# All low parts of the fp32r splits on VectorE instead of GpSimd, in a fused recurrence with two feed-forward networks

## The chip, the cores and the metric

The kernel runs on one core of a Trainium2 chip. The metric is device time of one execution in microseconds, the median of several runs. Engines are called as in the profile: PE is TensorE, DVE VectorE, ACT ScalarE, POOL GpSimd, SP the engine that issues the DMAs.

## The reference

```python
def _attn_ref(q, k, v, a_re, a_im):                # 4 batches, 8 heads, 768 steps, dim 48
    mag = np.sqrt(a_re * a_re + a_im * a_im)
    scale = np.minimum(mag, 0.999) / (mag + 1e-06)
    a_re_n, a_im_n = (a_re * scale, a_im * scale)
    for t in range(S):
        ar, ai = (a_re_n[:, :, t, :, None], a_im_n[:, :, t, :, None])
        new_re = ar * S_re - ai * S_im
        new_im = ar * S_im + ai * S_re
        S_re, S_im = (new_re + kv_t, new_im)       # kv_t: outer product of k and v of step t
        y[:, :, t] = q_t @ S_re

x = y as 3072 tokens x 384
x = (silu(x @ w_gate) * (x @ w_val)) @ w_out       # 384 -> 1536 -> 384
h = x @ w_in                                       # 384 -> 2048
return (h - np.tanh(h)) @ w_out2                   # 2048 -> 384, float32
```

The weights of both networks are drawn as 64-bit floats.

## The kernel before

**Splits.** A number that goes into a matmul of the two networks is held as two fp32r numbers, a high and a low part: ACT casts the value to fp32r (hi), and a subtraction, value minus hi, gives lo. Every product of two such numbers is three matmuls (hi.hi, hi.lo, lo.hi). The program makes a split in three kinds of places:

- `split` (lines 512 to 515) for the middle values: in network 1 after the gate product (L563), once per block of 128 of the 1536 columns and per token tile; in network 2 after `shrink` (lines 566 to 584, h - tanh h by five VectorE instructions L579, L581, L582, L583, L584). The cast is L514, the low part L515 on GpSimd. Only the very last one of the program was on VectorE (L640).
- `decode` (lines 146 to 161) for weights: `words` makes an fp32 out of the two 32-bit words of a double by ACT (L140) and four VectorE instructions in place on one tile (L141 to L144), then ACT casts (L150) and GpSimd subtracts (L152). For the first gate/value blocks TensorE makes the low part by two matmuls instead (L158, L159); that stays.
- The inputs of the networks (L464, L544) had their low part on VectorE already.

**Stages.** (1) Attention in chunks of 128 steps: `group_steps` makes the running products of the complex factors for two units (chunk of one batch) with VectorE products (L266, L268, L269) and a normalisation (squares L229 and the product L250 on GpSimd); `unit_a` and `unit_b` make scores, mask them (for the first eight units by GpSimd, L424), update the state (H products on GpSimd, L413 to L415) and write the unit's output as network 1's input. (2) Network 1 over ten token tiles of 256 (six) and 384 (four) tokens, `moe1_tile`: 12 steps per tile, each with 18 matmuls of the first product and 9 of the second for the step before. The attention of later tiles is put between its steps by `bg`, the decode of w_out in the first tile, and the decode of network 2's weights in the last tile (`dec2`), where raw tiles have three buffers and decoded ones two. (3) Network 2 over eight tiles of 384 tokens, `moe2_tile`: 16 steps per tile, each with 9 matmuls of the first product and 9 of the second, two steps behind. The rest of the decode of its second weights lies beside its first steps.

**The order of the work** is set by a scheduler which simulates the program as it is written and places each instruction in its engine's queue; each queue then runs in order on the chip. So a change of one instruction's engine moves others as well.

Of the kernel before, what the change touches and what calls it, by code (L numbers as in the profile page):

```python
# [8 lines left out]
F32 = mybir.dt.float32  # L9
# [4 lines left out]
ALU = mybir.AluOpType  # L14
# [27 lines left out]
def tile_kernel(ctx: ExitStack, tc: tile.TileContext, q, k, v, a_re, a_im, w_gate, w_val, w_out, w2_in, w2_out, out):  # L42
    nc = tc.nc
    PE, ACT, DVE, POOL, SP = nc.tensor, nc.scalar, nc.vector, nc.gpsimd, nc.sync
    B, H, S, D = q.shape
    NT, DM = out.shape
# [9 lines left out]
    NF2 = FF2 // P  # L56
# [12 lines left out]
    NTOK = 3 * P  # L69
# [58 lines left out]
    def PA(name):  # L128
        pool, tag = banks[0]
        banks.append(banks.pop(0))  # L130
        return pool.tile([P, 512], F32, tag=tag, name=name)
# [5 lines left out]
    def words(raw, t):  # L137

        w, ti = raw.bitcast(I32).rearrange("p (c w) -> p c w", w=2), t.bitcast(I32)
        ACT.activation(out=t, in_=raw.bitcast(F32).rearrange("p (c w) -> p c w", w=2)[:, :, 1], func=AF.Abs)  # L140
        DVE.tensor_scalar(out=t, in0=t, scalar1=W_LO, scalar2=W_HI, op0=ALU.max, op1=ALU.min)  # L141
        DVE.tensor_scalar(out=ti, in0=ti, scalar1=3, scalar2=0x3FFFFFF8, op0=ALU.logical_shift_left, op1=ALU.bitwise_and)  # L142
        DVE.scalar_tensor_tensor(out=ti, in0=w[:, :, 1], scalar=-0x40000000, in1=ti, op0=ALU.bitwise_and, op1=ALU.bitwise_or)  # L143
        DVE.scalar_tensor_tensor(out=ti, in0=w[:, :, 0], scalar=29, in1=ti, op0=ALU.logical_shift_right, op1=ALU.bitwise_or)  # L144

    def decode(raw, hi, lo, t, by_pe=False):

        words(raw, t)
        tv = t.rearrange("p (k c) -> p k c", c=hi.shape[2]) if len(hi.shape) == 3 else t
        ACT.copy(out=hi, in_=tv)  # L150
        if not by_pe:
            POOL.tensor_tensor(out=lo, in0=tv, in1=hi.bitcast(F32), op=ALU.subtract)  # L152
            return

        h2, l2 = (x.rearrange("p k c -> p (k c)") for x in (hi, lo))
        for c in range(0, t.shape[1], DM):
            ps = ps_1.tile([P, 512], F32, tag="l1", name="psL")[:, 0:DM]
            PE.matmul(ps, lhsT=ident, rhs=t[:, c:c + DM], start=True, stop=False)  # L158
            PE.matmul(ps, lhsT=nident, rhs=h2[:, c:c + DM], start=False, stop=True)  # L159
            ACT.copy(out=l2[:, c:c + DM], in_=ps)  # L160
# [346 lines left out]
    def catch_up(lag):  # L507

        while len(pend) > lag:
            pend.popleft()()  # L510

    def split(t, hi, lo, eng=POOL):

        ACT.copy(out=hi, in_=t)  # L514
        eng.tensor_tensor(out=lo, in0=t, in1=hi.bitcast(F32), op=ALU.subtract)  # L515

    def MT(tag, bufs, dt=F32):
        return m1.tile([P, N1], dt, tag=tag, name=tag, bufs=bufs)
# [51 lines left out]
    def shrink(p, t, pool):  # L570


        n = [P, p.shape[1]]
        uu = pool.tile(n, F32, tag="uu", name="uu")
        vv = pool.tile(n, F32, tag="vv", name="vv")
        far = pool.tile(n, I32, tag="far", name="far")
        ACT.activation(out=t, in_=p, func=AF.Tanh)  # L577
        ACT.activation(out=uu, in_=p, func=AF.Square, scale=KSQ)  # L578
        DVE.tensor_tensor(out=p, in0=p, in1=t, op=ALU.subtract)  # L579
        ACT.activation(out=vv, in_=uu, func=AF.Square, scale=1.0 / G_C, bias=gbias)  # L580
        DVE.tensor_scalar(out=far, in0=uu, scalar1=G_C * G_MAX * G_MAX, scalar2=None, op0=ALU.is_gt)  # L581
        DVE.tensor_tensor(out=t, in0=uu, in1=t, op=ALU.mult)  # L582
        DVE.scalar_tensor_tensor(out=t, in0=vv, scalar=G_F, in1=t, op0=ALU.add, op1=ALU.mult)  # L583
        DVE.copy_predicated(out=t, mask=far, data=p)  # L584
# [22 lines left out]
    def moe2_tile(ti, bg):  # L607
        x = ot.pop(ti)
        acc = []

        def l4(f, g):
            if f == 0:
                for n in range(ti * TU2, (ti + 1) * TU2):
                    acc.append((ps_2.tile([P, 512], F32, tag="l2", name="l4") if n % 5 < 3 else PA("l4"))[:, 0:DM])
            for tb in range(TU2):
                for n, (a, b) in enumerate(PASSES):
                    PE.matmul(acc[tb], lhsT=g[a][:, tb * P:(tb + 1) * P], rhs=w2_hl[f][:, b], start=(f == 0 and n == 0), stop=(f == NF2 - 1 and n == 2))  # L617
            if f == NF2 - 1:
                for tb in range(TU2):
                    r = m2.tile([P, DM], F32, tag="res", name="res", bufs=3)  # L620
                    with tc.high_priority():
                        if (ti + 1) * NTOK == NT and tb % 2:
                            DVE.tensor_copy(out=r, in_=acc[tb])
                        else:
                            ACT.copy(out=r, in_=acc[tb])
                    row = ti * NTOK + tb * P
                    SP.dma_start(out=out[row:row + P, :], in_=r)

        for f in range(NF2):
            sl = slice(f * P, (f + 1) * P)  # L630
            pool, tag = (ps_1, "l1") if f % 3 < 2 else (ps_g, "psA")
            p = pool.tile([P, 512], F32, tag=tag, name="l3")[:, 0:NTOK]
            for n in range(3 * NJ):
                kk, (a, b) = n // 3, PASSES[n % 3]
                PE.matmul(p, lhsT=wi_hl[a][:, kk, sl], rhs=x[b][:, kk, :], start=(n == 0), stop=(n == 3 * NJ - 1))  # L635
            catch_up(2)
            t = MT("t", MID)[:, 0:NTOK]
            shrink(p, t, m2)
            g = [MT(tag, MID, F32R)[:, 0:NTOK] if f % (MID + 2) < MID else m2.tile([P, NTOK], F32R, tag=tag, name=tag) for tag in ("hi", "lo")]
            split(t, *g, eng=DVE if (ti + 1) * NTOK == NT and f == NF2 - 1 else POOL)  # L640
            pend.append(lambda f=f, g=g: l4(f, g))
            bg(f)

# [59 lines left out]
    for ti in range(len(TILES)):  # L703
# [11 lines left out]
        def bg(n):  # L715
            if ti == 0:
                dec1(N_PRE + 2 + n)
            if last:
                if n == 2 * N_A:
                    w1a.close()  # L720
                    w2.append(second.enter_context(tc.tile_pool(name="w2a", bufs=1, side="left", reuse_waits="tile")))
                if n < NF2:
                    dec2(n, "i")
                for _ in range(W2STEP):
                    if n >= N0 and len(w2_hl) < N_EARLY + (2 * N_A if n >= 2 * N_A else 0):
                        get_w2()
            prog["credit"] += RATE
            while prog["credit"] >= 1:
                prog["credit"] -= 1
                att_next(goal, SHARE if ti else SHARE1)  # L730
# [170 lines left out]
```

## Time and profile before

| | |
|---|---|
| three runs | 1281.08 us median (1279.9 to 1281.22) |
| the profiled execution | 1280.44 us in all, span 1278.7 us |
| PE busy | 1147.8 us, 90% of the span |
| DVE busy | 1008.1 us, 79%, 1961 instructions |
| ACT busy | 695.3 us, 54% |
| POOL busy | 465.8 us, 36%, 402 instructions |
| DMA | 163.53 MB, 128 GB/s mean |

Busy time is the union of an engine's instructions as the profiler recorded them, from start to end, whatever an instruction did in between. Shares of the whole span are means over stages with different limits, so the rows by stage tell more.

### The profile page before, as it was taken

To read this page: it belongs to the slowest core of one execution; us is meant where nothing else is said; L and a number is where in the kernel's file an instruction comes from. 1 tells how busy PE (TensorE), PEld (TensorE's weight loads), DVE (VectorE), ACT (ScalarE), POOL (GpSimd) and SP (SyncE) were. 2 spreads that over 40 slices of the span, in tenths; PEclk is the share of its full clock that TensorE was granted. 3 is DMA by queue.
4 is the path that set the end of the run, shared out by engine and by line. 5 is a ranking of instruction groups with operands and counts; after the bars stand their busy time and mean duration, and the time that the engine had idled before them with its cause. 6 is when DMAs were issued, how large, how long until landed. Compare 5 with 4: busy or idle time off the path is not lost.

```text
span 1278.7 us, 21147 instructions
## 1 busy us (share of the span) xinstructions
PE 1147.8 (90%) x7512; PEld 1113.6 (87%) x7512; DVE 1008.1 (79%) x1961; ACT 695.3 (54%) x1454; POOL 465.8 (36%) x402
## 2 busy tenths in 40 slices
PE   3346899898999999999999998987999999999997
PEld 2126888898999998999999998877999999999996
DVE  6988988697675849677683328999998899999996
ACT  6454655556545463736534224446666566666664
POOL 0034454333252223233232224544444444444442
PEclk9755979999899999999999999998999999999999
DMA  6586667679676776768565546752101101101000
GB/s 169 141 203 146 145 185 194 158 194 215 158 176 178 183 186 151 184 155 185 160 145 141 147 118 221 235 173 87 57 1 57 38 20 56 38 19 56 1 19 22
DMA packets 282289, 163.53 MB, mean 128 GB/s; under 512 B 155328, under 2 KB 263232, under 8 KB 282176
## 3 DMA queue, kind: packets, MB, share of 16 engines
q1 hardware_dynamic: 282176, 162.10, 48.7%
q8 instruction: 61, 1.00, 0.3%
q14 instruction: 52, 0.43, 0.1%
HBM read 121.26 MB, written 37.86 MB: 124 GB/s over the span
## 4 chain that ended last, share of the span: by engine, by line
PE 53%; DVE 23%; ACT 8%; DMA 8%; issue 4%; POOL 2%; SPq 1%; DVEq 0%; ACTq 0%; POOLq 0%
PE l L617 14%; PE l L635 13%; PE l L554 12%; PE acc L538 5%; PE psS L420 2%; DVE prod L266 2%; DVE t L143 2%; DMA TQ<-qk_d 2%; PE psY L448 2%; DVE PL L268 2%; PE psY L446 2%; DVE t L142 1%; DVE t L583 1%; DVE t L144 1%; DMA raw<-in_moe_w_val_dram 1%
## 5 line engine op out<-in xcount | busy, mean ns | idle before, releaser
L515 POOL TENSOR_TENSOR lo<-t,hi 128x384 fp32r<-128x384 f32 (+1 forms) x247 | 289.4, 1172 | 517.2 <-ACT hi L514 485.7
L554 PE MATMUL l<-x,wgv 128*128 128x256 f32 (+1 forms) x2160 | 366.8, 317 | 21.6 <-DVE t L563 14.6
L554 PEld LDWEIGHTS l<-x,wgv 128*128 128x128 f32 x2160 | 324.4, 197 | 29.4 <-DVE t L563 19.4
L514 ACT CAST hi<-t 128x384 fp32r<-128x384 f32 (+1 forms) x248 | 119.5, 482 | 244.4 <-DVE t L563 141.6
L635 PE MATMUL l<-x,wi 128*128 128x384 f32 x1152 | 223.0, 339 | 8.3 <-DVE t L584 7.2
L635 PEld LDWEIGHTS l<-x,wi 128*128 128x128 f32 x1152 | 202.5, 189 | 9.9 <-DVE t L584 8.3
L617 PE MATMUL l<-w,hi 128*128 128x384 f32 x768 | 188.0, 338 | 0.5 <-ACT hi L514 0.5
L538 PE MATMUL acc<-hi,wo 128*128 128x256 f32 (+1 forms) x720 | 180.0, 312 | 4.0 <-ACT hi L514 2.7
L583 DVE SCALAR_TENSOR_TENSOR t<-vv,t 128x384 f32<-128x384 f32 x128 | 139.8, 1092 | 11.8 <-DVE t L582 0.5
L617 PEld LDWEIGHTS l<-w,hi 128*128 128x128 f32 x768 | 139.5, 189 | 0.8 <-ACT hi L514 0.8
L538 PEld LDWEIGHTS acc<-hi,wo 128*128 128x128 f32 x720 | 127.0, 193 | 5.8 <-ACT hi L514 3.8
L617 PE MATMUL l<-w,lo 128*128 128x384 f32 x384 | 120.2, 337 | 0.0
L563 DVE TENSOR_TENSOR t<-t,l 128x256 f32<-128x256 f32 (+1 forms) x120 | 56.2, 468 | 81.0 <-PE l L554 67.8
L538 PE MATMUL acc<-lo,wo 128*128 128x256 f32 (+1 forms) x360 | 111.3, 315 | 3.8 <-POOL lo L515 3.8
L266 DVE TENSOR_TENSOR prod<-PL 128x384 f32<-128x384 f32 x168 | 111.6, 664 | 3.1
L577 ACT ACTIVATE t<-l 128x384 f32<-128x384 f32 x128 | 62.9, 491 | 50.4 <-PE l L635 48.1
L579 DVE TENSOR_TENSOR l<-l,t 128x384 f32<-128x384 f32 x128 | 72.1, 563 | 13.1 <-ACT uu L578 13.1
L580 ACT ACTIVATE vv<-uu,gbias 128x384 f32<-128x384 f32 x128 | 79.4, 621 | 0.4
L558 ACT ACTIVATE t<-l 128x256 f32<-128x256 f32 (+1 forms) x120 | 51.1, 426 | 51.7 <-PE l L554 50.9
L584 DVE COPY_PREDICATED t<-far,l 128x384 f32<-128x384 int32 x128 | 75.8, 592 | 3.7
L446 PE MATMUL psY<-v,SC 128*128 128x48 f32 x384 | 75.3, 291 | 0.7 <-POOL SC L424 0.6
L538 PEld LDWEIGHTS acc<-lo,wo 128*128 128x128 f32 x360 | 69.2, 192 | 6.0 <-POOL lo L515 5.7
(131 smaller groups left out, 1936.8 us busy)
## 6 DMA issues: line engine op xcount, KB each, us to landing
wo<-wo_d SPq DMA_DIRECT2D x108, 384.0 KB, 3.9
qk_d<-QK SPq DMA_DIRECT2D x24, 768.0 KB, 4.6
raw<-in_moe_w_out_dram SPq DMA_DIRECT2D x28, 384.0 KB, 3.1
TK<-qk_d SPq DMA_DIRECT2D x48, 192.0 KB, 4.2
TQ<-qk_d SPq DMA_DIRECT2D x48, 192.0 KB, 5.1
x<-o_d SPq DMA_DIRECT2D x16, 576.0 KB, 5.2
raw<-in_moe_w_in_dram SPq DMA_DIRECT2D x16, 384.0 KB, 3.8
ar<-in_a_re_dram SPq DMA_DIRECT2D x24, 192.0 KB, 3.8
```

The source lines that it names most:

```text
L266: DVE.tensor_tensor(out=pr, in0=prev.unsqueeze(2).to_broadcast(sh), in1=cur.unsqueeze(1).to_broadcast(sh), op=ALU.mult)
L446: PE.matmul(o, lhsT=SC[h // 4][:, h % 4], rhs=vn[:, D * h:D * (h + 1)], start=True, stop=(c == 0))
L514: ACT.copy(out=hi, in_=t)
L515: eng.tensor_tensor(out=lo, in0=t, in1=hi.bitcast(F32), op=ALU.subtract)
L538: PE.matmul(acc[j], lhsT=w[:, a, j * P:(j + 1) * P], rhs=m[b], start=(f == 0 and i == 0), stop=(f == NF1 - 1 and i == 2))
L554: PE.matmul(p, lhsT=w[a][:, kk], rhs=x[b][:, kk, 0:n_t], start=(n == 0), stop=(n == 3 * NJ - 1))
L579: DVE.tensor_tensor(out=p, in0=p, in1=t, op=ALU.subtract)
L580: ACT.activation(out=vv, in_=uu, func=AF.Square, scale=1.0 / G_C, bias=gbias)
L583: DVE.scalar_tensor_tensor(out=t, in0=vv, scalar=G_F, in1=t, op0=ALU.add, op1=ALU.mult)
L584: DVE.copy_predicated(out=t, mask=far, data=p)
L617: PE.matmul(acc[tb], lhsT=g[a][:, tb * P:(tb + 1) * P], rhs=w2_hl[f][:, b], start=(f == 0 and n == 0), stop=(f == NF2 - 1 and n == 2))
L635: PE.matmul(p, lhsT=wi_hl[a][:, kk, sl], rhs=x[b][:, kk, :], start=(n == 0), stop=(n == 3 * NJ - 1))
```

## The change

`decode` and `split` call VectorE for the subtraction; the argument that chose the engine goes, and with it the exception for the last step. The matmul form of the low part stays, as do the other GpSimd instructions.

```diff
@@ decode
         ACT.copy(out=hi, in_=tv)
         if not by_pe:
-            POOL.tensor_tensor(out=lo, in0=tv, in1=hi.bitcast(F32), op=ALU.subtract)
+            DVE.tensor_tensor(out=lo, in0=tv, in1=hi.bitcast(F32), op=ALU.subtract)
             return
@@ split
-    def split(t, hi, lo, eng=POOL):
+    def split(t, hi, lo):
         ACT.copy(out=hi, in_=t)
-        eng.tensor_tensor(out=lo, in0=t, in1=hi.bitcast(F32), op=ALU.subtract)
+        DVE.tensor_tensor(out=lo, in0=t, in1=hi.bitcast(F32), op=ALU.subtract)
@@ moe2_tile
-            split(t, *g, eng=DVE if (ti + 1) * NTOK == NT and f == NF2 - 1 else POOL)
+            split(t, *g)
```

The scheduler places the moved instructions, and others with them. Three places:

GpSimd's queue at the start, before (wo and wgv are decoded weights of network 1, SC the scores, ar a factor of the recurrence):

```order
L152 TENSOR_TENSOR wo<-dt,wo 128x384
L229 TENSOR_TENSOR s_516<-s_516,s_517 128x768
L152 TENSOR_TENSOR wo<-dt,wo 128x384
L152 TENSOR_TENSOR wgv_143<-dt,wgv_142 128x768
L424 AFFINE_SELECT SC<-SC 128x512
L250 TENSOR_TENSOR ar<-ar,s_516 128x768
L424 AFFINE_SELECT SC<-SC 128x512
L152 TENSOR_TENSOR wo<-dt,wo 128x384
```

and after the change:

```order
L229 TENSOR_TENSOR s_516<-s_516,s_517 128x768
L424 AFFINE_SELECT SC<-SC 128x512 x2
L250 TENSOR_TENSOR ar<-ar,s_516 128x768
L413 TENSOR_TENSOR Hn<-Z,LS 96x384
L414 TENSOR_TENSOR Zs<-Zs,LS 96x384
```

The low parts are gone from it, and both masks of the first unit stand ahead of the normalisation.

VectorE's queue in the last tile of network 1, one step from L563 to L563, before (t_ are tiles under decode, raw_ the raw words):

```order
L563 TENSOR_TENSOR t<-t,l_8964 128x384
L141 TENSOR_SCALAR t_9221<-t_9221 128x384
L142 TENSOR_SCALAR t_9221<-t_9221 128x384
L143 SCALAR_TENSOR_TENSOR t_9221<-raw_9220,t_9221 128x384
L141 TENSOR_SCALAR t_9258<-t_9258 128x384
L144 SCALAR_TENSOR_TENSOR t_9221<-raw_9220,t_9221 128x384
L142 TENSOR_SCALAR t_9258<-t_9258 128x384
L143 SCALAR_TENSOR_TENSOR t_9258<-raw_9257,t_9258 128x384
L563 TENSOR_TENSOR t<-t,l_9026 128x384
```

and after the change, two steps later:

```order
L563 TENSOR_TENSOR t<-t,l_9084 128x384
L144 SCALAR_TENSOR_TENSOR t_9258<-raw_9257,t_9258 128x384
L141 TENSOR_SCALAR t_9269<-t_9269 128x384
L515 TENSOR_TENSOR lo<-t,hi 128x384
L142 TENSOR_SCALAR t_9269<-t_9269 128x384
L152 TENSOR_TENSOR w_9256<-t_9258,w_9256 128x384
L143 SCALAR_TENSOR_TENSOR t_9269<-raw_9268,t_9269 128x384
L144 SCALAR_TENSOR_TENSOR t_9269<-raw_9268,t_9269 128x384
L141 TENSOR_SCALAR t_9292<-t_9292 128x384
L563 TENSOR_TENSOR t<-t,l_9132 128x384
```

Low parts of the middle values and of the weights now stand between the decode's instructions, and a step holds a little less of the decode: when the last L563 is reached, 3 decodes more than before are still to be done, beside the first steps of network 2.

VectorE's queue in the steady loop of network 2, one step, before:

```order
L582 TENSOR_TENSOR t<-uu,t 128x384
L583 SCALAR_TENSOR_TENSOR t<-vv,t 128x384
L584 COPY_PREDICATED t<-far,l_10429 128x384
L579 TENSOR_TENSOR l_10464<-l_10464,t 128x384
L581 TENSOR_SCALAR far<-uu 128x384
```

and after the change:

```order
L582 TENSOR_TENSOR t<-uu,t 128x384
L515 TENSOR_TENSOR lo<-t,hi 128x384
L583 SCALAR_TENSOR_TENSOR t<-vv,t 128x384
L584 COPY_PREDICATED t<-far,l_10429 128x384
L579 TENSOR_TENSOR l_10464<-l_10464,t 128x384
L581 TENSOR_SCALAR far<-uu 128x384
```

The low part of the step before now stands between L582 and L583 of the next one.

## Rows read from the trace of the kernel before

**Rows 1.** Busy time of the engines by stage, us from the span's start
```profile
core 0: us, PE busy (x) PEld busy (x) DVE busy (x) ACT busy (x) POOL busy (x), PEclk, DMA share, GB/s
0.00:135.00 135.00, 63.06 (x246) 46.71 (x246) 106.70 (x222) 72.85 (x139) 32.29 (x30) 0.70 0.65 163
135.00:560.00 425.00, 392.92 (x3159) 385.47 (x3157) 328.76 (x714) 237.80 (x506) 159.73 (x148) 0.95 0.73 179
560.00:764.00 204.00, 203.81 (x1361) 201.75 (x1360) 106.86 (x233) 85.97 (x172) 54.28 (x50) 0.97 0.58 144
764.00:890.00 126.00, 108.40 (x578) 100.71 (x577) 115.23 (x189) 62.78 (x134) 58.30 (x54) 0.97 0.58 188
890.00:1260.00 370.00, 370.00 (x2125) 370.00 (x2125) 342.06 (x593) 230.73 (x495) 158.02 (x119) 1.00 0.09 31
```

**Rows 2.** Groups of GpSimd's instructions by line and shape: busy us, mean ns | idle before
```profile
L515 POOL TENSOR_TENSOR lo<-t,hi 128x384 fp32r<-128x384 f32 x175 | 223.0, 1274 | 359.5 <-ACT hi L514 328.0 <-issue 9.3 <-PE l L635 6.9
L515 POOL TENSOR_TENSOR lo<-t,hi 128x256 fp32r<-128x256 f32 x72 | 66.4, 922 | 157.8 <-ACT hi L514 157.8
```

**Rows 3.** Groups of VectorE's instructions by line, whole span: busy us, mean ns | idle before
```profile
L583 DVE SCALAR_TENSOR_TENSOR t<-vv,t 128x384 f32<-128x384 f32 x128 | 139.8, 1092 | 11.8 <-DVE t L582 0.5
...
L143 DVE SCALAR_TENSOR_TENSOR t<-raw,t 128x384 int32<-128x384 int32 x32 | 29.4, 917 | 1.0
L144 DVE SCALAR_TENSOR_TENSOR t<-raw,t 128x384 int32<-128x384 int32 x32 | 23.6, 738 | 0.7
...
L142 DVE TENSOR_SCALAR t<-t 128x384 int32<-128x384 int32 x32 | 20.8, 651 | 0.7
...
L515 DVE TENSOR_TENSOR lo<-t,hi 128x384 fp32r<-128x384 f32 x1 | 0.6, 559 | 0.6 <-ACT hi L514 0.6
```

**Rows 4.** Timeline of network 2's loop: start us, duration us, engine, line, instruction
```profile
1004.27 0.56 DVE L579 TENSOR_TENSOR l<-l,t 128x384 f32<-128x384 f32 x1
...
1005.01 0.55 DVE L582 TENSOR_TENSOR t<-uu,t 128x384 f32<-128x384 f32 x1
1005.06 1.38 POOL L515 TENSOR_TENSOR lo<-t,hi 128x384 fp32r<-128x384 f32 x1 [1.72 <-ACT hi L514]
...
1005.66 1.19 DVE L583 SCALAR_TENSOR_TENSOR t<-vv,t 128x384 f32<-128x384 f32 x1
...
1007.37 0.56 DVE L579 TENSOR_TENSOR l<-l,t 128x384 f32<-128x384 f32 x1
...
1224.46 0.55 DVE L583 SCALAR_TENSOR_TENSOR t<-vv,t 128x384 f32<-128x384 f32 x1
```

**Rows 5.** Timeline of one step of the decode beside network 1's last tile
```profile
839.55 0.55 DVE L563 TENSOR_TENSOR t<-t,l 128x384 f32<-128x384 f32 x1
840.01 1.21 DVE L142 TENSOR_SCALAR t<-t 128x384 int32<-128x384 int32 x1
...
843.40 0.36 DVE L142 TENSOR_SCALAR t<-t 128x384 int32<-128x384 int32 x1
843.72 1.00 POOL L152 TENSOR_TENSOR w<-t,w 128x384 fp32r<-128x384 f32 x1 [1.64 <-ACT w L150]
843.80 1.34 DVE L143 SCALAR_TENSOR_TENSOR t<-raw,t 128x384 int32<-128x384 int32 x1
...
845.91 0.55 DVE L563 TENSOR_TENSOR t<-t,l 128x384 f32<-128x384 f32 x1
```

**Rows 6.** Timeline of GpSimd at the start
```profile
90.42 6.50 POOL L152 TENSOR_TENSOR wgv<-dt,wgv 128x768 fp32r<-128x768 f32 x1 [4.70 <-ACT wgv L150]
96.86 1.36 POOL L424 TENSOR_SCALAR_AFFINE_SELECT SC<-SC 128x512 f32<-128x512 f32 x1
...
100.26 0.96 POOL L424 TENSOR_SCALAR_AFFINE_SELECT SC<-SC 128x512 f32<-128x512 f32 x1
```

**Rows 7.** Groups of VectorE's instructions by line, 135 to 560 us
```profile
L266 DVE TENSOR_TENSOR prod<-PL 128x384 f32<-128x384 f32 x112 | 76.3, 681 | 2.1
L268 DVE TENSOR_TENSOR PL<-prod 128x96 f32<-128x96 f32 x111 | 44.6, 401 | 1.4
```

**Rows 8.** Instructions of line 268: ns least/median/most, first and last start
```profile
L268 DVE TENSOR_TENSOR PL<-prod x168: 240/256/1896, 31.3 to 666.7; 128x96 f32<-128x96 f32 x168
```

## The prediction

> **What bounds the kernel now.** I read the busy time of each engine by stages first. The reader is to see five stretches with five limits [rows 1]. Up to 135 us TensorE works less than half the time: the first attention units and the first weights are on their way. From 135 to 560 us (the six 256-token tiles) it is busy 392.9 of 425 us, VectorE 328.8. From 560 to 764 it is full (203.8 of 204) and VectorE half idle. From 764 to 890 (the second network's weights are decoded) VectorE is the fullest at 115.2 of 126, and TensorE leaves 17.6 us unused. From 890 on TensorE is busy 370.00 of 370 us with 2125 matmuls, 174 ns each. A step of network 2 has 18 of them, so 3.13 us.
>
> So a change to VectorE and GpSimd can win at most where TensorE is not full: some 72 us in the first stretch, 32 in the second, 17.6 in the fourth, and the end. It can lose anywhere, if VectorE becomes slower than TensorE.
>
> Then I read how long the same VectorE instruction takes at different times. L583 takes 1092 ns on average [rows 3], 1.19 us in the steady loop, but 0.55 us at 1224.46, in a pause of GpSimd's low parts [rows 4]. In the loop it starts at 1005.66 while GpSimd's low part runs from 1005.06 to 1006.44, and it ends at 1006.85, 0.41 us after that part: it stands still behind it. The decode shows the same: L142 takes 0.36 us alone and 1.21 us at 840.01; L143 takes 1.34 us at 843.80, beside a low part that runs to 844.72, and ends 0.42 us after it [rows 5]. The two engines do not work side by side here; an instruction of one waits for one of the other. GpSimd's busy time is thus largely VectorE's too.
>
> **The change part by part.** It removes 294 subtractions from GpSimd (247 of L515 and 47 of L152) and puts them on VectorE. GpSimd needs 1274 ns for the 384-wide and 922 for the 256-wide ones [rows 2]. VectorE has one such instruction in the trace, the last of the program: 559 ns for 384 columns [rows 3]. Independent instructions follow each other faster than they take: L579 at 1004.27 takes 0.56, L582 at 1005.01 takes 0.55, yet L579, L581 and L582 start within 0.74 us [rows 4]. I cost a 384-wide low part at 0.47 us of VectorE's queue, with 0.56 as the upper bound; the 256-wide ones at 0.35, between 256/384 of 0.559 (0.37) less the overlap, and 0.56 above.
>
> *Network 2's loop (890 us to the end).* One VectorE step is L579 to L579, 1004.27 to 1007.37, or 3.10 us [rows 4]: hardly less than TensorE's 3.13. Without GpSimd, L583 falls from 1.19 to 0.55, which returns 0.64; the low part costs 0.47 to 0.56. The step becomes 2.93 to 3.02 us, and the new order puts the low part behind L582, three instructions after the L584 whose result ScalarE casts for it, so that the cast lies beside them. TensorE stays the bound: 0 us for 118 steps. At the very end L583 and L579 of the last step come some 0.5 us sooner: -0.5.
>
> VectorE is busy 342 of 370 us in this stretch [rows 1], so it looks like the engine to take work from. The Trainium skill (Perfetto Trace Analysis, Optimizing Scalar/DVE Operations) says that where VectorE is saturated, moving work to ScalarE or even GpSimd may pay, with the caution that those two share a port. By its first half this change goes the wrong way, and the sum would be that of the second rival below; by the rows of L583 it costs nothing.
>
> *The decode (764 to 890 us).* Here VectorE is the bound, and its own waits behind GpSimd can be counted from the 32 decodes [rows 3]: L142 651 instead of 360 ns (9.3 us), L143 917 instead of 550 (11.7), L144 738 instead of 550 (6.0); the short times are those of L142 at 843.40 and of L583 at 1224.46, which is the same operation on as many columns [rows 4, 5]. Together 27 us come back. Added are the low parts that GpSimd did in this window, 54 instructions [rows 1], at 0.47 us: 25.4 us. The difference is -1.6 us. But the low parts also fill gaps. The decode's four instructions work in place on one tile, so each waits for the one before: L142 at 843.40 takes 0.36 and the next starts 0.40 later, and L143 alone would hold the queue 0.55 to 0.6 us before L144 [rows 5]. The new order puts low parts between them. With some 0.1 us saved at two places of each of 32 decodes, 6.4 us more. I take -7. The bounds: TensorE cannot gain more than the 17.6 us it leaves here, so -17.6; and if the low parts take 0.56 (30.2 us) and a third of them wait 0.5 us for their cast (9 us), +12.
>
> A step of network 1's last tile shows the size: L563 at 839.55 to L563 at 845.91 is 6.36 us [rows 5], against 27 matmuls of 174 ns, 4.70 us, for TensorE. The new order has three decodes fewer before the last L563 than the old one, and so three more beside network 2's first steps; the sum over the whole window holds both.
>
> *The start (0 to 135 us).* GpSimd's low part of a whole gate/value block runs from 90.42 for 6.50 us, and the mask of the first scores (L424) follows it at 96.86, the second at 100.26 behind the normalisation L250 [rows 6]. In the new order the two masks stand first. That can bring the first unit forward by 0 to 6.5 us; six low parts on VectorE (three of them twice as wide) cost 3 x 1.1 + 3 x 0.56 = 5 us at most, beside other work and waits for loads. I take -3, with -6.5 and +5 as bounds.
>
> *The 256-token tiles (135 to 560 us).* Added: 72 low parts of 0.35 and nine of L152 at 0.47, 29 us. Returned: L268 takes 401 ns on average against a median of 256 over the kernel, 111 times, 16.1 us [rows 7, 8]; L266 681 ns against the 559 of the low part that has its size [rows 3, 7], 112 times, 13.7 us. But of GpSimd's 159.7 us here the low parts are 66 to 76 (72 of 922 ns and nine more), under half, and the masks, the H products and the normalisation stay. So some 13 of those 30 us return, and VectorE has some 16 us more to do in a stretch where it idles 96. For it: GpSimd's remaining work no longer queues behind low parts. I take 0, with -10 (a third of TensorE's 32 idle us) and +12.
>
> From 560 to 764 us TensorE is full and VectorE has 97 us to spare for its 20-odd low parts: 0. No DMA is added. GpSimd issues none; SP's stores of the decoded weights wait for VectorE instead.
>
> **The sum**: -0.5 - 7 - 3 + 0 = -10.5 us against the profiled execution (1278.7 us span, 1280.44 in all), 1269.9 us. That execution lies 0.64 under the median of 1281.08, so the same change gives 1270.5 there: I say 1270.
>
> **The rivals.** *One: the gain is only moved.* The decode's raw tiles have three buffers, and a load can start only after the L144 three decodes before. Loads then set the pace, or the three decodes pushed behind the last L563 take back what the earlier steps gained. The decode gives 0, the start 0 to 3: 1277 to 1281. For it: TensorE waits at the border of the two networks for VectorE in any case. Against it: L141 to L144 hardly wait for loads in this trace. Chance 0.13.
>
> *Two: VectorE saturates.* If L583, L142 and L143 are long for a reason of their own, the loop becomes 3.10 + 0.47 = 3.57 us against 3.13, and 118 steps cost 52 us; the decode adds 25: 1357 us. It decides as soon as L583 stays above 1.0 us. The short L583 at 1224.46 speaks against it. The rule on saturated engines would have it so. Chance 0.04.
>
> *Three: VectorE becomes the bound in the 256-token tiles.* Its queue is in order, and a low part waits there for ScalarE's cast, with the attention's products behind it. If the 13 us do not return, since the remaining GpSimd work now hits VectorE instead, 29 us are added, on the path in the share in which VectorE is busy, 329 of 425: +22, less 10.5: 1292 us. It turns to slower when more than 10.5 of the 29 us reach the end. For it: VectorE is on the chain at several places there. Against: 96 us idle. Chance 0.11.
>
> **How the numbers follow.** The forecast has 0.72, of which 0.70 ends faster and 0.02 within 0.2% (2.6 us, about what a measurement of this kernel can tell from no change). Rival one's 1277 to 1281 lies across that line: 0.06 faster, 0.07 same. Rival three: 0.03 same, 0.08 slower; rival two: 0.04 slower. Faster 0.76, same 0.12, slower 0.12. The range: the bounds of decode, start and tiles add to -34 and +29, which won't meet; two of three at the good end give -25 (1255), and toward the other side the range takes in rival one and a little of three, 1284.
>
> **What would show it.** Right: in the steady loop L583 at 0.55 us and the step of TensorE at 3.13; L142 to L144 near 0.36 and 0.55; the stretch from the first decode to the first full step of network 2 shorter by 4 to 12 us; the first masks 2 to 6 us earlier. Wrong: L583 still above 1 us; VectorE at over 95% between 135 and 560 us and TensorE's idle time there above 40 us; or steps of network 2 over 3.2 us.

## The result, and the profile after

The changed kernel takes 1243.89 us (median of 4 runs, 1241.27 to 1248.19), the kernel before beside it 1281.15 us. The ratio is 0.972 with a 95% interval of 0.9689 to 0.9751: 37 us faster. The forecast of 1270 us had the direction right and the size wrong; even its low end, 1255, was too high. The profiled execution took 1244.15 us with a span of 1242.4 us, 36.3 less than before.

The page's first rows, which answer to the table of before:

```profile
PE 1131.6 (91%) x7512; PEld 1100.3 (89%) x7512; DVE 989.9 (80%) x2255; ACT 693.9 (56%) x1454; POOL 124.2 (10%) x108
```

VectorE executes 294 instructions more and is busy 18 us less (989.9 against 1008.1). To see where the 36.3 us lie, both traces have to be cut at the same points of the work, not at the same times. The marks are the starts of VectorE instructions: the first L563 (network 1 begins), the 37th (its fourth tile), the 73rd (its seventh, the first of 384 tokens), the last L464 (the attention's last output), the first L584 (the first finished middle value of network 2) and the last L584. The view of busy time by stretch, of the kernel before, cut there:

```profile
0.00:137.00 137.00, 65.06 (x262) 48.71 (x263) 108.11 (x224) 74.44 (x143) 32.29 (x30) 0.70 0.66 163
137.00:347.70 210.70, 190.46 (x1499) 185.32 (x1499) 170.30 (x367) 124.94 (x263) 86.57 (x80) 0.94 0.72 177
347.70:541.90 194.20, 184.18 (x1532) 182.48 (x1532) 139.19 (x313) 105.03 (x228) 64.13 (x61) 0.97 0.73 180
541.90:764.60 222.70, 220.70 (x1478) 218.03 (x1477) 124.75 (x266) 92.69 (x186) 63.31 (x56) 0.97 0.60 149
764.60:868.40 103.80, 87.66 (x473) 80.59 (x471) 93.99 (x150) 50.85 (x108) 48.95 (x46) 0.99 0.63 205
868.40:1267.00 398.60, 397.15 (x2265) 396.51 (x2266) 370.00 (x642) 245.94 (x527) 170.52 (x129) 0.99 0.11 35
```

And of the changed kernel (columns as in [rows 1]: the stretch, its length, then busy us and instructions of PE, PEld, DVE, ACT and POOL, granted clock, DMA share, GB/s):

```profile
0.00:135.30 135.30, 66.46 (x256) 47.61 (x257) 107.73 (x227) 72.22 (x137) 16.47 (x24) 0.68 0.64 163
135.30:329.30 194.00, 180.68 (x1501) 177.62 (x1501) 165.62 (x400) 118.12 (x253) 46.54 (x36) 0.97 0.76 189
329.30:527.70 198.40, 185.45 (x1544) 181.99 (x1542) 145.91 (x362) 114.71 (x245) 31.68 (x25) 0.98 0.76 182
527.70:747.10 219.40, 217.62 (x1476) 214.64 (x1477) 134.00 (x302) 92.73 (x185) 29.53 (x24) 0.99 0.62 152
747.10:831.60 84.50, 80.67 (x464) 79.75 (x462) 77.35 (x183) 48.56 (x101) 0.00 (x0) 0.99 0.75 238
831.60:1231.80 400.20, 397.68 (x2261) 395.99 (x2262) 357.56 (x786) 246.19 (x533) 0.00 (x0) 0.99 0.11 36
```

The differences are -1.7, -16.7, +4.2, -3.3, -19.3 and +1.6 us, and the work behind the last mark is 1.1 us shorter (11.7 against 10.6): -36.3 together. Two places carry it: the six 256-token tiles of network 1, and the border between the networks, where the weights are decoded. The six tiles are to be read together, -12.5 us, since some of the attention's work has moved across the mark between the third and the fourth: of L347, for example, four instructions stood in the first three tiles, and three do now. At the border TensorE's idle time falls from 16.1 us (103.80 less 87.66) to 3.8, at a granted clock of 0.99 before and after.

The reader is to see VectorE's column. At the border it executes 183 instructions in place of 150 and is busy 17 us *less*. In the six tiles it is 82 instructions more (762 against 680) and only 2.0 us more (311.5 against 309.5). VectorE's groups over the whole span, which answer to [rows 3, 7, 8], show why:

```profile
L266 DVE TENSOR_TENSOR prod<-PL 128x384 f32<-128x384 f32 x168 | 100.1, 596 | 2.9
L515 DVE TENSOR_TENSOR lo<-t,hi 128x384 fp32r<-128x384 f32 x176 | 98.9, 562 | 21.0 <-ACT hi L514 20.9
L583 DVE SCALAR_TENSOR_TENSOR t<-vv,t 128x384 f32<-128x384 f32 x128 | 70.4, 550 | 0.8
...
L515 DVE TENSOR_TENSOR lo<-t,hi 128x256 fp32r<-128x256 f32 x72 | 39.1, 543 | 11.2 <-ACT hi L514 10.9
L143 DVE SCALAR_TENSOR_TENSOR t<-raw,t 128x384 int32<-128x384 int32 x32 | 17.7, 553 | 0.2
L144 DVE SCALAR_TENSOR_TENSOR t<-raw,t 128x384 int32<-128x384 int32 x32 | 17.7, 552 | 0.3
...
L142 DVE TENSOR_SCALAR t<-t 128x384 int32<-128x384 int32 x32 | 11.3, 355 | 0.3
```

L583 is at 550 ns where it was at 1092, L143, L144 and L142 at 553, 552 and 355 where they were at 917, 738 and 651. A low part takes 562 ns here; on GpSimd it took 1274 [rows 2]. In the timeline of VectorE in network 2's loop (which answers to [rows 4]) no instruction is lengthened any more, and a step, from the L579 at 1000.63 to that at 1003.73, has room for 0.41 us of idle time:

```profile
1000.63 0.56 DVE L579 TENSOR_TENSOR l<-l,t 128x384 f32<-128x384 f32 x1
1001.10 0.34 DVE L581 TENSOR_SCALAR far<-uu 128x384 int32<-128x384 f32 x1
...
1002.30 0.54 DVE L515 TENSOR_TENSOR lo<-t,hi 128x384 fp32r<-128x384 f32 x1
1002.77 0.54 DVE L583 SCALAR_TENSOR_TENSOR t<-vv,t 128x384 f32<-128x384 f32 x1
1003.73 0.57 DVE L579 TENSOR_TENSOR l<-l,t 128x384 f32<-128x384 f32 x1 [0.41 <-ACT uu L578]
```

A step of network 1's last tile beside the decode (which answers to [rows 5]; timeline of VectorE, some lines left out) shows every instruction at its short duration, and all but two start before the one ahead has ended. Its length, 4.44 us from L563 to L563, is no measure of the gain against the 6.36 quoted before: the steps of that tile are uneven (0.46 to 6.37 us before, 0.07 to 6.81 after; their means are 3.75 and 4.45 us), and the decode that they hold differs. The border's whole length is the measure.

```profile
799.22 0.55 DVE L563 TENSOR_TENSOR t<-t,l 128x384 f32<-128x384 f32 x1
799.68 0.35 DVE L142 TENSOR_SCALAR t<-t 128x384 int32<-128x384 int32 x1
799.95 0.55 DVE L152 TENSOR_TENSOR w<-t,w 128x384 fp32r<-128x384 f32 x1
800.42 0.55 DVE L143 SCALAR_TENSOR_TENSOR t<-raw,t 128x384 int32<-128x384 int32 x1
800.89 0.55 DVE L515 TENSOR_TENSOR lo<-t,hi 128x384 fp32r<-128x384 f32 x1
...
803.66 0.55 DVE L563 TENSOR_TENSOR t<-t,l 128x384 f32<-128x384 f32 x1
```

### The profile page after: what moved, and what is told of

Same layout as the page of the kernel before. It is cut to its first block, busy times and chain, and to the rows that moved or that the text cites. A ratio compares the mean times of both kernels' runs of the same rounds, so it can differ in the third digit from the quotient of the medians.

```text
span 1242.4 us, 20766 instructions
## 1 busy us (share of the span) xinstructions
PE 1131.6 (91%) x7512; PEld 1100.3 (89%) x7512; DVE 989.9 (80%) x2255; ACT 693.9 (56%) x1454; POOL 124.2 (10%) x108
## 4 chain that ended last, share of the span: by engine, by line
PE 62%; DVE 15%; ACT 12%; DMA 8%; issue 2%; SPq 1%; ACTq 0%; DVEq 0%
PE l L635 15%; PE l L617 15%; PE l L554 15%; PE acc L538 7%; PE psS L420 3%; DMA TQ<-qk_d 2%; DVE prod L266 2%; DMA qk_d<-QK 1%; DVE PL L268 1%; ACT NW L313 1%; PE psY L448 1%; DVE lo L515 1%; PE psY L446 1%; DVE QK L376 1%; DMA raw<-in_moe_w_val_dram 1%
## 5 line engine op out<-in xcount | busy, mean ns | idle before, releaser
L554 PE MATMUL l<-x,wgv 128*128 128x256 f32 (+1 forms) x2160 | 361.4, 313 | 11.6 <-ACT t L558 7.5
L554 PEld LDWEIGHTS l<-x,wgv 128*128 128x128 f32 x2160 | 320.6, 194 | 14.9 <-ACT t L558 8.7
L635 PE MATMUL l<-x,wi 128*128 128x384 f32 x1152 | 223.1, 338 | 6.3 <-DVE t L584 5.7
L635 PEld LDWEIGHTS l<-x,wi 128*128 128x128 f32 x1152 | 202.4, 189 | 8.4 <-DVE t L584 7.4
L617 PE MATMUL l<-w,hi 128*128 128x384 f32 x768 | 178.4, 338 | 0.0
L538 PE MATMUL acc<-hi,wo 128*128 128x256 f32 (+1 forms) x720 | 175.8, 309 | 0.6 <-DMA wo<-wo_d 0.6
L515 DVE TENSOR_TENSOR lo<-t,hi 128x384 fp32r<-128x384 f32 (+1 forms) x248 | 138.0, 556 | 32.2 <-ACT hi L514 31.8
L538 PEld LDWEIGHTS acc<-hi,wo 128*128 128x128 f32 x720 | 125.0, 191 | 0.9 <-issue 0.8
L538 PE MATMUL acc<-lo,wo 128*128 128x256 f32 (+1 forms) x360 | 109.6, 310 | 1.8 <-DVE lo L515 1.6
L617 PE MATMUL l<-w,lo 128*128 128x384 f32 x384 | 110.4, 337 | 0.0
L563 DVE TENSOR_TENSOR t<-t,l 128x256 f32<-128x256 f32 (+1 forms) x120 | 56.2, 469 | 60.0 <-PE l L554 43.4
L266 DVE TENSOR_TENSOR prod<-PL 128x384 f32<-128x384 f32 x168 | 100.1, 596 | 2.9
L579 DVE TENSOR_TENSOR l<-l,t 128x384 f32<-128x384 f32 x128 | 72.2, 564 | 35.4 <-ACT uu L578 34.3
L420 PE MATMUL psS<-TQ,TK 96*128 96x128 f32 x384 | 55.9, 296 | 27.1 <-DMA TQ<-qk_d 25.7
L420 PEld LDWEIGHTS psS<-TQ,TK 96*128 96x128 f32 x384 | 52.1, 209 | 29.0 <-issue 21.8
L584 DVE COPY_PREDICATED t<-far,l 128x384 f32<-128x384 int32 x128 | 75.7, 592 | 2.5
L538 PEld LDWEIGHTS acc<-lo,wo 128*128 128x128 f32 x360 | 68.7, 191 | 2.7 <-DVE lo L515 2.7
```

The source lines that it names most:

```text
L266: DVE.tensor_tensor(out=pr, in0=prev.unsqueeze(2).to_broadcast(sh), in1=cur.unsqueeze(1).to_broadcast(sh), op=ALU.mult)
L420: PE.matmul(ps[:, P * i:P * (i + 1)], lhsT=TK[:, 4 * hh + i], rhs=TQ[:, 4 * hh + i], start=True, stop=True)
L515: DVE.tensor_tensor(out=lo, in0=t, in1=hi.bitcast(F32), op=ALU.subtract)
L538: PE.matmul(acc[j], lhsT=w[:, a, j * P:(j + 1) * P], rhs=m[b], start=(f == 0 and i == 0), stop=(f == NF1 - 1 and i == 2))
L554: PE.matmul(p, lhsT=w[a][:, kk], rhs=x[b][:, kk, 0:n_t], start=(n == 0), stop=(n == 3 * NJ - 1))
```

## The experiments

Three theories could explain the 36 us. A: VectorE's instructions had been lengthened behind GpSimd's subtractions, and this time came back. B: the planner's new order did it, or shorter waits for GpSimd's results. C: TensorE's clock, through fewer gaps. The table gives the length of each stretch between the marks in each profiled run, in us; the last column is the ratio to the kernel before, run beside it.

| run | to 1st L563 | tiles 1-3 | tiles 4-6 | tiles 7 to last L464 | border | loop | ratio, 95% interval |
|---|---|---|---|---|---|---|---|
| before | 137.0 | 210.7 | 194.2 | 222.7 | 103.9 | 398.6 | 1 |
| after | 135.3 | 194.0 | 198.4 | 219.5 | 84.4 | 400.2 | 0.972, 0.9689-0.9751 |
| e1 decode on GpSimd | 137.8 | 201.7 | 191.2 | 218.0 | 91.1 | 400.2 | 0.9844, 0.98-0.9889 |
| e2 network 1 on GpSimd | 136.8 | 202.4 | 204.5 | 223.1 | 89.6 | 398.0 | 0.9864, 0.9847-0.9882 |
| e3 network 2 on GpSimd | 136.6 | 194.4 | 197.9 | 220.2 | 84.1 | 401.7 | 0.976, 0.9738-0.9783 |
| e4 doubled | 138.6 | 210.7 | 200.8 | 223.2 | 100.0 | 419.7 | 1.0209, 1.0189-1.0228 |
| e5 reads in the loop | 135.3 | 195.5 | 196.6 | 219.9 | 84.6 | 426.6 | 0.9944, 0.9922-0.9966 |
| e6 zeros written | 136.2 | 200.1 | 193.8 | 216.6 | 84.7 | 402.5 | 0.9784, 0.9748-0.982 |
| e7 all arithmetic | 134.7 | 199.5 | 188.7 | 220.7 | 84.5 | 400.2 | 0.9683, 0.9657-0.971 |
| e10 masks too | 133.6 | 208.6 | 196.1 | 221.4 | 87.2 | 399.7 | 0.9808, 0.9778-0.9839 |
| e11 after, again | 136.7 | 192.6 | 201.8 | 217.8 | 83.9 | 400.2 | 0.9729, 0.9702-0.9756 |
| e12 as e7, again | 134.2 | 198.6 | 187.1 | 218.8 | 83.6 | 400.2 | 0.9653, 0.9632-0.9673 |
| e8 before, other order | 128.9 | 267.7 | 234.6 | 220.4 | 112.7 | 436.1 | 1.1087, 1.1041-1.1133 |
| e9 after, other order | 127.7 | 258.5 | 224.6 | 217.6 | 92.3 | 396.6 | 1.0401, 1.037-1.0432 |

A row is one execution. Those of e2 (1266.22 us) and e10 (1259.04) were the longest of their four, that of e1 (1252.16) one of two short ones.

The sum of the six tiles sorts the runs: 404.9, 406.9 and 411.5 us where GpSimd subtracts behind every middle value of network 1 (before, e2, e4), and 392.1 to 394.4 in the runs where it does not and its other work in the attention stands (after, e1, e3, e5, e6, e11).

### Undoing one part: e1, e2, e3

Each run is the changed kernel with one kind of low part given back to GpSimd.

```diff
 # e1, decode:
-            DVE.tensor_tensor(out=lo, in0=tv, in1=hi.bitcast(F32), op=ALU.subtract)
+            POOL.tensor_tensor(out=lo, in0=tv, in1=hi.bitcast(F32), op=ALU.subtract)
 # e2, moe1_tile (split gets its argument eng back):
-            split(s, *m)
+            split(s, *m, eng=POOL)
 # e3, moe2_tile (all but the last):
-            split(t, *g)
+            split(t, *g, eng=DVE if (ti + 1) * NTOK == NT and f == NF2 - 1 else POOL)
```

> The changed kernel, with the low parts of the decoded weights alone (47 subtractions, L152) given back to GpSimd; the middle values of both networks stay on VectorE. Theory A (VectorE's instructions were lengthened behind GpSimd's subtractions, and each low part given back brings its own share): most of the 18 us that the decode stretch of the second network (764 to 890 before) gave comes back, since 32 of the 54 low parts there are decodes: 1244 + 10 to 18, I take 1257, and the first 135 us lose up to 2 us. Theory B (the planner's new order, or GpSimd's shorter queue, made the gain): no such place; within 5 us of 1244. Theory C (TensorE's clock, through fewer gaps in the 256-token tiles): the middle stretch keeps its 12 us and the granted clock there stays near 0.98.

> The changed kernel, with the low parts of network 1's middle values alone (120 subtractions, all between 137 and 764 us) given back to GpSimd. Theory A: the 256-token tiles (135 to 560 before) lose the 12.5 us and 560 to 764 the 3 us that they gained: 1244 + 12 to 16, I take 1258; L583 and the decode behind 764 stay as in the changed kernel. Theory B (order or queue): the planner makes a third order here, so the loss may have either sign and any place. Theory C: the loss is there and goes with a granted clock that falls from 0.98 to about 0.95 in the middle stretch.

> The changed kernel, with the low parts of network 2's middle values alone (128 subtractions less the last, L515 behind 764 us) given back to GpSimd. Theory A: the loop (118 steps behind 890 us) is bound by TensorE at 3.10 us a step and loses nothing; of the 18 us of the decode stretch (764 to 890), where 22 of the 54 low parts are middle values, 3 to 8 us come back: 1244 + 3 to 8, I take 1249. If the loop itself slows by over 0.03 us a step (over 4 us), my term 0 for it was wrong. Theory B: within 5 us, with either sign.

Measured: 1256.30, 1261.94 and 1246.49 us, where A took 1257, 1258 and 1249 (the kernel before took 1278.00 beside them). The three losses against the ratio 0.972 are 0.0124, 0.0144 and 0.004, together 0.031, against the whole 0.028: the parts nearly add up.

The places are partly others than A said. e2 loses 14.5 us in the six tiles (A had 12.5), 3.6 in the tiles after them, and 5.2 at the border, by the blocks of network 1 that still run there. e1 loses 6.7 us at the border, where A had most of 10 to 18, and 0.5 in the six tiles, in spite of its nine decodes there; of its 12 us by the median the profiled execution shows only 8. e3 gives nothing back at the border, where A, counting the loop's first steps in, had 3 to 8. So of the 19.5 us that the border gained, e1 and e2 take back 11.9; the rest is seen only where GpSimd has all of them. Network 2's loop is 1.5 us longer in e3, of 400, although L583 is back at a mean of 1074 ns: the last term of the forecast that was 0 stands.

C has no part at the border, where the granted clock is 0.99 before and after. In the tiles its sign came: the clock in tiles 4 to 6 of e2 is 0.94 in place of 0.98. There the clock goes with the low parts, but not with them alone, since the changed kernel itself has 0.96 in e11; what lowers it was not tried.

```profile
136.80:339.10 202.30, 183.43 (x1488) 178.12 (x1489) 168.33 (x376) 120.02 (x257) 81.34 (x72) 0.97 0.71 175
339.10:543.60 204.50, 192.23 (x1549) 189.90 (x1548) 143.85 (x318) 112.05 (x241) 64.65 (x62) 0.94 0.76 184
```

In these two rows of e2 VectorE executes 694 instructions in 312.2 us of busy time, where the changed kernel executes 762 in 311.5: the 68 that it is spared save it nothing.

### GpSimd works, nobody reads it: e4 and e6

e4 keeps every low part on VectorE and lets GpSimd make the same subtraction once more behind it, in place on a tile that nothing reads afterwards. e6 has two writings of zeros in its place.

```diff
 # in decode and in split, behind VectorE's subtraction (t is tv in decode):
+        POOL.tensor_tensor(out=t, in0=t, in1=hi.bitcast(F32), op=ALU.subtract)    # e4
+        POOL.memset(t, 0.0); POOL.memset(t, 0.0)                                  # e6
```

> The changed kernel, and behind each low part of a split GpSimd makes the same subtraction once more, into the middle value's or decoded word's own tile (in place), which nothing reads afterwards: GpSimd's reading and writing as in the kernel before, at the same places, while no reader waits for it. Theory A (contention): all the 37 us come back and VectorE, which keeps its low parts as well, becomes the bound in the second network's loop: 328 us busy of 370 after, plus the 70 us by which its instructions were lengthened there before, 398 against 370, so 1244 + 37 + 28: 1290 to 1315, I take 1305. Theory B (who waits for GpSimd's queue, or the planner's order): nobody waits for the extra work, so 1244 within 6.

> As the kernel with the doubled subtraction, but in its place GpSimd sets the same tile to zero twice: the tile is held and GpSimd is used at the same places, yet it reads nothing. Theory A1 (what cost the time is GpSimd's two-input subtraction beside VectorE, and in the loop the held tile): up to 890 us the time is that of the changed kernel within 8 us, the loop loses up to 20: 1244 to 1270, I take 1256. Theory A2 (the held tiles, or any work of GpSimd on these tiles): as with the doubled subtraction, 1290 to 1310.

Measured: 1304.44 us for e4 (A took 1305) and 1249.78 us for e6 (A1 took 1256). Up to the first L584 e4 gives back more than the gain: that mark stands at 873.2 us, where it stood at 868.5 before and at 831.6 after the change. The six tiles take 411.5 us (404.9 before), the border 100.0 (103.9 before), though no instruction of TensorE or VectorE reads what GpSimd makes. With e6 GpSimd holds the same tiles and is nearly as busy there (36.8 us at the border for 42.9), and the border stays at 84.7 us, the six tiles at 393.9. The rows of the border, e4 first, then e6:

```profile
773.20:873.20 100.00, 85.37 (x465) 79.59 (x464) 96.46 (x166) 44.20 (x95) 42.94 (x39) 0.99 0.58 188
746.70:831.30 84.60, 80.60 (x463) 79.67 (x462) 77.06 (x171) 44.44 (x97) 36.77 (x80) 0.99 0.72 228
```

VectorE is busy 96.46 us with 166 instructions in the one and 77.06 with 171 in the other; L143 has a mean of 716 ns in e4 and 555 in e6 there, the low part L515 853 and 556. ScalarE's waits for tiles that GpSimd still holds are the same in both up to the first L584 (L140, 23.2 us in e4 and 23.6 in e6). So the price lies in GpSimd's two-input subtraction running beside VectorE, not in held tiles and not in waits for its results; of the latter TensorE had 3.8 us in all (L538, 5 times) between 137 and 868 us in the kernel before. The Trainium skill (SBUF - State Buffer, Who interferes with whom) says just this: a VectorE instruction with two inputs in SBUF contends with a GpSimd instruction that reads SBUF, and not with one that only writes it. These two runs agree. That sentence does not cover L142, L141 and L581, which have one input tile and were lengthened in the kernel before all the same (means of 651, 458 and 442 ns around the border, 355, 355 and 349 after).

In e4's loop the 20 us came about differently than A had it. VectorE's L583 and L515 stay short there (558 and 556 ns, 127 times each), and what is new is ScalarE's wait for the tile that GpSimd still holds, in the view of waits of e4 from 873.2 us on (engine and line waiting, releaser, us in total, times, longest):

```profile
ACT t L577 <- PE l L635: 60.9, 59, 1.6
ACT hi L514 <- DVE t L584: 48.5, 59, 1.9
ACT t L577 <- POOL t L515: 37.4, 26, 2.9
```

So the right total of e4 is in part a coincidence: its loop has a wait of the experiment's own. The next run is free of that.

### Reads in the loop alone: e5

```diff
 # in moe2_tile, behind split:
+            junk = m2.tile([P, NTOK], F32, tag="junk", name="junk", bufs=1)
+            POOL.tensor_tensor(out=junk, in0=g[0].bitcast(F32), in1=g[0].bitcast(F32), op=ALU.subtract)
```

> The changed kernel, and in the second network's 128 steps GpSimd subtracts the high part from itself, as soon as it is there, into a scratch tile of its own: nobody reads that, nothing waits for it, and no tile is held longer than TensorE holds it. Theory A (VectorE's instruction that runs beside GpSimd's subtraction is lengthened): L583 goes back from 0.55 to about 1.09 us in the loop, VectorE has 0.33 us of idle time a step left there, so a step grows by 0.2 to 0.55 us: 118 steps give 21 to 65 us, I take 35: 1279. Theory B (lengthening came from VectorE and GpSimd waiting for each other's results): L583 stays at 0.55 us and the time within 3 of 1244.

Measured: 1271.36 us, in A's range and 8 under its value. All of it lies in the loop, 426.6 us against 400.2. VectorE's groups in the loop of e5, and its busy time there:

```profile
L515 DVE TENSOR_TENSOR lo<-t,hi 128x384 fp32r<-128x384 f32 x127 | 120.4, 948 | 4.4 <-ACT hi L514 4.4
...
L583 DVE SCALAR_TENSOR_TENSOR t<-vv,t 128x384 f32<-128x384 f32 x127 | 70.9, 558 | 0.8
...
L581 DVE TENSOR_SCALAR far<-uu 128x384 int32<-128x384 f32 x126 | 54.6, 433 | 0.0
```
```profile
831.90:1258.50 426.60, 410.50 (x2268) 394.68 (x2268) 417.40 (x786) 248.32 (x533) 130.48 (x127) 0.99 0.10 34
```

It is not L583 that is lengthened here, as A had said, but L515 (948 ns for 550) and some of L581 (433 for 349): in the timeline, the instruction that comes next in VectorE's queue when GpSimd begins. VectorE is busy 417.4 of 426.6 us and has become the bound. The changed loop is thus within 0.33 us a step (400.20 less 357.56 us, by 128) of VectorE's limit, and one GpSimd subtraction a step costs VectorE 0.47 (417.40 less 357.56, by 128). The timeline of e5 shows one such case, and that it is a wait: GpSimd's subtraction ends at 1005.53, the low part 0.41 us later.

```profile
1004.68 0.85 POOL L640 TENSOR_TENSOR junk<-hi 128x384 f32<-128x384 f32 x1 [1.47 <-ACT hi L514]
...
1004.75 1.19 DVE L515 TENSOR_TENSOR lo<-t,hi 128x384 fp32r<-128x384 f32 x1
```

### Another order: e8 and e9

Both kernels were ordered by the planner's other cost table.

```diff
-    with _tile.TileContext(nc, schedule_with_timeline_sim=True) as tc:
+    with _tile.TileContext(nc, schedule_with_timeline_sim=False) as tc:
```

> The kernel before, with the planner told to order by another cost table (one argument of the tile context), so that each engine's instructions stand in another order than in either kernel. By itself it says nothing; its time, which I expect between 1275 and 1310, is the base for the next run.

> The changed kernel with the same other order of planning. Theory A (returned waits, whatever the order): against the run before it the gain is again 25 to 45 us. Theory B (the order that the planner chose with the change made the gain): less than 12 us, or a loss.

Measured: 1416.64 and 1331.07 us. The other order is far worse for both (my 1275 to 1310 for the first was wrong by over 100 us), and the gain in it is 85.6 us, nearly twice A's upper figure. So the direction does not hang on one order, but the size does: network 2's loop, which gained nothing in the real case, takes 436.1 us in e8 (first to last L584) and 396.6 in e9. The border gains 20.4 us in this order too (112.7 to 92.3), and the six tiles 19.2. How much of the 36 us came from the order that the planner chose was not separated further.

### Going on: e7, e10, and e7 again

e7 moves the rest of GpSimd's arithmetic to VectorE too; e10 also the masks of the first eight units.

```diff
 # e7
-                squares(POOL)
+                squares(DVE)
-                norm(POOL)
+                norm(DVE)
-            POOL.tensor_tensor(out=heads(Hn), in0=heads(Z), in1=lam(0), op=ALU.mult)
+            DVE.tensor_tensor(out=heads(Hn), in0=heads(Z), in1=lam(0), op=ALU.mult)
...
 # e10, on top
-    NORM_AT, NA0, SCM = 5, 1, 8
+    NORM_AT, NA0, SCM = 5, 1, 0
```

> The changed kernel, and all of GpSimd's other arithmetic (L413 to L415, L229, L250: 80 instructions, 109 us of GpSimd) made by VectorE too; GpSimd keeps the 16 masks (L424) and the start. Theory A: some 52 us of new VectorE work (60 of about 0.55 us, 20 of about 0.96 us) stand against the roughly 45 us by which its instructions are still lengthened behind GpSimd before 764 us, and the results come sooner (0.55 for 1.1 us): 1244 less 0 to 8, I take 1240. Rival (VectorE, 329 of 410 us in the tiles now, becomes the bound there): 1247 to 1260.

> The kernel in which VectorE makes all of GpSimd's arithmetic, and now also the masks of the first 8 units (16 times 0.69 us on VectorE, in place of a copy of 0.58 us on ScalarE and 0.91 us on GpSimd): GpSimd has nothing left behind the start. Theory A: 11 us more of VectorE's work against the last lengthened instructions and a shorter way for 16 masks: within 4 us of 1239, I take 1238. Rival (VectorE is the bound in the first 210 us): 1243 to 1252.

> The changed kernel itself, on the same chip and beside the same runs as the next one. Every theory: 0.972 of the kernel before, within 0.003 (1241 to 1248).

> The kernel in which VectorE makes all of GpSimd's arithmetic but the 16 masks, once more, to tell its 5 us of gain over the changed kernel from chance. Theory A (the last lengthened instructions are worth a few us): 3 to 7 us under the run beside it, 0.968 of the kernel before. Rival (the planner's order alone moves the time by so much): the same figures cannot tell them apart, but a difference under 2 us would mean that there was none.

Measured: e7 1238.86 us; beside each other e11 (the changed kernel) 1244.81, ratio 0.9729 (0.9702 to 0.9756), and e12 (as e7) 1235.48, ratio 0.9653 (0.9632 to 0.9673). The intervals don't meet, so e7 beats both kernels, by 45 and 9 us. It wins in the six tiles (385.7 us in e12, 394.4 in e11; the first three lose 6.0, the next gain 14.7). In tiles 4 to 6 VectorE again does more instructions (394 against 362) in hardly more busy time, as the row of e12 shows beside that of the changed kernel from 329.3:

```profile
332.80:519.90 187.10, 182.36 (x1534) 180.26 (x1532) 147.46 (x394) 109.95 (x238) 0.00 (x0) 0.98 0.80 192
```

e10 missed both figures with 1255.90 us. Its loss lies mostly in the tiles (208.6 for 199.5 and 196.1 for 188.7 us), with VectorE busy 168.0 of 208.6 us, so it is not full; the granted clock in the first of them is 0.93, for 0.96 in e7. Whether the masks' place in VectorE's queue or the new order costs it was not tried. Taking the last work from GpSimd is no gain as such, and since e10's six tiles, without any work of GpSimd, take 404.7 us, as long as before the change, something else than the low parts can cost as much there.

## Why the prediction was wrong

| term | forecast | measured |
|---|---|---|
| start | -3 | -1.7 |
| 256-token tiles | 0 | -16.7 + 4.2 = -12.5 |
| 560 to 764 us | 0 | -3.3 |
| decode, to the steady loop | -7 | -19.3 + 1.6 = -17.7 |
| network 2's loop | 0 | 0 (in the row above) |
| end | -0.5 | -1.1 |

**The mechanism was right.** VectorE waited behind GpSimd [rows 3 to 5]; e4, e5 and e6 show it. The sum was undersized at two terms, the decode and the tiles.

**The decode: -7 was mis-sized.** The step was "together 27 us come back", counted from L142, L143 and L144 alone. These three gave just that: 73.8 us of durations became 46.7. But the low parts also hit the instructions that run between them. VectorE's groups from the last L464 to the 17th L584, of the kernel before:

```profile
L583 DVE SCALAR_TENSOR_TENSOR t<-vv,t 128x384 f32<-128x384 f32 x17 | 17.6, 1033 | 1.4
L141 DVE TENSOR_SCALAR t<-t 128x384 f32<-128x384 f32 x32 | 14.7, 458 | 5.3 <-ACT t L140 4.7 <-DMA raw<-in_moe_w_in_dram 0.6
...
L581 DVE TENSOR_SCALAR far<-uu 128x384 int32<-128x384 f32 x17 | 7.5, 442 | 0.0
```

and of the changed kernel:

```profile
L583 DVE SCALAR_TENSOR_TENSOR t<-vv,t 128x384 f32<-128x384 f32 x17 | 9.3, 548 | 0.1
...
L581 DVE TENSOR_SCALAR far<-uu 128x384 int32<-128x384 f32 x17 | 5.9, 349 | 0.0
```

L583 gives 8.3 us, L141 3.3 (its 32 took 355 ns each after), L581 1.6: 13.2 us that I left out, half as much again as the 27 that I counted, with L583's own short time standing in [rows 4]. Then the low parts: 64 here, 35.2 us by their durations (32 of L515, 17.6; 32 of L152, 8.8 twice). Durations fall by 5.1 us; VectorE's busy time falls by 15.2 (143.62 to 128.47), so 10 us more come from instructions that overlap, for which I had 6.4. VectorE also idles 3.5 us less (11.6 to 8.1). Together 18.6 us, about the 17.6 that TensorE left unused: my lower bound was the result. With the 13 us counted I would have forecast about -20, held at -17.6. (My two figures, -1.6 and -6.4, add to -8.0; I took -7.) The step of 6.36 us that I showed was a long one, above the mean of 3.75 in that tile.

**The 256-token tiles: 0 was wrong.** The step was "so some 13 of those 30 us return, and VectorE has some 16 us more to do". I scaled the lengthening by GpSimd's busy share and looked at two lines only. VectorE did all of the 81 low parts (72 of 0.54 us and nine of L152) in 2.0 us more busy time than before: of the 29 us that I had added, some 27 came back, not 13. They lie in L266, L268 (447 to 398 ns in the first three tiles), L269 (319 to 261), in the decode of w_out (L143, 860 to 547), and in long instructions such as L249. VectorE's groups in the first three tiles, of the kernel before:

```profile
L266 DVE TENSOR_TENSOR prod<-PL 128x384 f32<-128x384 f32 x56 | 38.4, 686 | 1.0
...
L249 DVE SCALAR_TENSOR_TENSOR ai<-ai,sgn,s 128x768 f32<-128x768 f32 x4 | 8.2, 2061 | 0.0
```

and of the changed kernel:

```profile
L266 DVE TENSOR_TENSOR prod<-PL 128x384 f32<-128x384 f32 x56 | 32.9, 588 | 0.9
...
L249 DVE SCALAR_TENSOR_TENSOR ai<-ai,sgn,s 128x768 f32<-128x768 f32 x4 | 4.4, 1106 | 0.0
```

Then TensorE gave a second part. In the six tiles it did 3031 and 3045 matmuls in 374.6 and 366.1 us: of the 12.5 us, 8.5 are shorter matmul time and only 4.0 less idle time. The granted clock (a mean over its two levels, 1.2 and 2.4 GHz) rose from 0.94 to 0.97 in the first three tiles and from 0.97 to 0.98 in the next. How the gain is shared between the two varies: the changed kernel has 370.1 us of matmul time and 24.3 of idle time there in e11. But TensorE's busy time is 374.6 to 375.7 in before, e2 and e4, and 365.4 to 370.1 in after, e1, e3, e5, e6 and e11. My bound of -10, a third of TensorE's idle time, took its busy time as fixed and had no place for that. That the granted clock rose because the gaps shrank was not tried.

**What was right.** The loop: L583 at 0.55 us, 0 us for 118 steps, and e3 shows that GpSimd may have these low parts or not. The start: the masks (L424) come at 95.87 and 97.57 us, 1.0 and 2.7 earlier; I had said 2 to 6, so the first falls short. The rivals fell: the raw loads don't set the pace at the border (no instruction of VectorE waits for one there after the change), L583 is short, VectorE is not above 95% in the tiles (311.5 of 392.4 us). The rule of the Trainium skill (Perfetto Trace Analysis, Optimizing Scalar/DVE Operations) that a saturated VectorE may be relieved by GpSimd would have gone the wrong way; its caution, that GpSimd and VectorE share a port, is what decided here.

## What to carry to other kernels

VectorE's busy time contained its waits behind GpSimd here. Before moving work off a full VectorE to GpSimd, compare each VectorE line's mean with its shortest duration, over *all* lines of the stretch: here each of the 64 low parts at the border had lengthened VectorE's work by some 0.63 us (40.3 us by 64), more than the 0.55 us that VectorE needs to make it. And TensorE's busy time was no fixed floor here: of the 12.5 us in the tiles, 8.5 came back from it (4.5 of 10.5 in e11), with a higher granted clock. Stretches are compared between marks that hold the same work.

## What the runs showed that was not expected

- The wait goes both ways. GpSimd's subtraction of 384 columns takes 0.83 us at the least (e5; 0.85 in the case shown, where VectorE's low part waits for it; the median of e5 is 1.12), 1.38 in [rows 4], and in e4's loop two of them together 3.11 us, while VectorE's low part and L583 beside them kept their 0.55:

```profile
1004.38 3.11 POOL L515 TENSOR_TENSOR t<-t,hi 128x384 f32<-128x384 f32 x2 [6.46 <-DVE lo L515]
...
1004.62 0.55 DVE L515 TENSOR_TENSOR lo<-t,hi 128x384 fp32r<-128x384 f32 x1
1005.09 0.55 DVE L583 SCALAR_TENSOR_TENSOR t<-vv,t 128x384 f32<-128x384 f32 x1
```

- GpSimd's writing of zeros beside VectorE lengthened nothing in the steady loop: L583 has a mean of 554 ns between 900 and 1200 us in e6, 551 in the changed kernel. The loop is 2.3 us longer.
- Four executions of the changed kernel lie at 1241.27, 1243.64, 1244.15 and 1248.19 us with granted clocks of 0.958, 0.954, 0.952 and 0.946: a spread of 7 us that goes with the clock. It does not always: of the five in e11 the longest, 1250.02, has 0.951, and that of 1245.31 has 0.946.
- The planner's cost table, one argument, is worth 137 us on the kernel before (1416.64 against 1279.54), more than three times the change studied here.
